# Batch 3's keys loaded behind group 1's last first-layer word, and seven more unread products in the opening of an attention and Fourier-mixing kernel

## The chip, the cores and the metric

The kernel runs on one core of one Trainium2 chip. The metric is the device time of one execution in microseconds; a kernel's time is the median of its runs. TensorE is written PE, VectorE DVE, ScalarE ACT, GpSimd POOL, and SyncE, which issues the DMA transfers, SP. PEld is PE's weight load and SPq is SP's queue.

## The reference, cut to what matters

Everything is in float32. Eight batches have 576 rows of 512 columns (eight heads of 64).

```python
q_s = softmax(q, over the 64 columns of a head)
k_s = softmax(k, over the 576 rows)
kv = einsum('bhsd,bhse->bhde', k_s, v)          # 64 x 64 per head
x = einsum('bhsd,bhde->bhse', q_s, kv)          # laid out as (8, 576, 512)
u = x + real(fft(fft(x, axis=1), axis=2))
un = (u - mean(u)) / sqrt(var(u) + 1e-6)        # over the 512 columns
out = u + relu(un @ w_ch1) @ w_ch2              # 512 -> 2048 -> 512
```

## The kernel before

**Order of the work.** Every step is a Python function with a time, in units close to a microsecond. All steps are sorted by time and recorded in that order, under a manual schedule, so each engine carries out its own instructions in the order of these times, and SP issues its transfers in that order too. A time in the code is a place in the order, not a moment on the chip. When a step really starts is set by semaphores: its operands, the buffer that it writes, and whatever stands ahead of it on its engine.

**Stages.** Batch 0 is worked off in an *opening* whose order is written out by hand in the string `OPENING`. Then come the two layers of group 0 as plain products (`plain`). While these run, the weights are put together for Strassen-like forms (seven products for eight) and written to DRAM as `w1s` and `w2s`. The groups 1 to 7 follow. Each has a first layer (`up`, products at line 1543) and a second (`down`; group 1's products are at line 1759, the others' at 1640 and 1670). While group g's layers run, the attention of the batch after it is worked off between their products.

**The opening, as far as it bears on the change.** SP loads the keys of batch 0 in four blocks, the rows shared by two batches, the queries of the tiles A to D (`own`), and the values in two halves. For each key block there is a maximum (DVE, line 553), an exponential (ACT, 556), a turn by four PE transposes (561), and a copy to SBUF (ACT, 564). `k0 last` (569) turns the last rows of all four blocks and `k0 fifth` (DVE, 572) copies them. The queries get a maximum (967), a subtraction (972, POOL or DVE), an exponential (ACT, 976), a turn (984) and a copy (995). The products of keys and values (585) need both halves of the values; `k0 scale` (DVE, 588) scales them, and the queries' products (839) need that. `t` stands for the shared rows. It has a sum and reciprocal (`t inverse`, DVE, 945 to 947), a scaling (956), a turn, folds on POOL (1017 to 1025) and products (839, 1060).

`WARM` lists unread products that are put into the opening: (time, number, columns). `warm` multiplies a block of ones by itself into a PSUM tile that nobody reads. The tile comes from `flat`, the pool `tr` of two buffers, which the transposes also use. In the opening `acc` gives a tile of the pool `two` of three buffers, which the other products use. A new tile in a pool waits until the last user of the buffer that it gets is done.

**Weights and keys in the groups.** The first layer of a group streams eight blocks of `w1s`, here called words 0 to 7, through four places in SBUF. When word n has been used, `used(n)` issues the load of word n + 4 (`load`, line 475). Words 6 and 7 are so issued as the second quarter of the first layer ends, and are needed at the start of its last quarter. `ahead(b)` puts the loads of batch b's keys (`keys_to`, four transfers, line 676), of the first half of its values (`values_to`, eight transfers, line 688) and of two query tiles at fixed times from the start of the group that runs before. Batch 3's are so loaded during group 1 and batch 4's during group 2. All are issued by SP, in one order:

```python
steps = at(20 if b == 2 else 27 if b < 5 else 24, self.keys_to(b))
steps += at(35 if b > 2 else 22.5, self.values_to(b, 0))
```

Word 6 is recorded at 27.5 of the group and word 7 at 32.5. SP waits in order: a transfer that is not yet allowed to start keeps those behind it back.

Of the kernel before, what the change touches and what calls it, by code (L numbers as in the profile page):

```python
# [46 lines left out]
P = 128  # L47
B, H, S, DH = 8, 8, 576, 64
D = H * DH
# [35 lines left out]
PAIRS = [(j + NP // 2, j) for j in range(NP // 2)]  # L85

DOWN = [(i, f) for n in range(4) for i in (2, 3, 0) for f in range(4 * n, 4 * n + 4)] + [(1, f) for f in range(NF)]
WARM = (2, 4, 256), (7.26, 1, 64), (8.52, 1, 64), (18.63, 2, 256), (22.111, 10, 256)
OPENING = """
4.30 k00 max, 5.10 k00 exp, 5.50 k01 max, 6.05 k00 turn, 6.30 k01 exp, 6.65 k02 max, 7.06 k00 four,  # L90
7.25 k01 turn, 7.56 k02 exp, 7.75 k03 max, 8.32 k01 four, 8.51 k02 turn, 8.82 k03 exp, 8.90 A max, 9.50 B max,
# [28 lines left out]
def at(t, script):  # L120
    return [(t + dt, step) for dt, step in script]
# [17 lines left out]
class _Block:  # L139
# [124 lines left out]

    def warm(self, n, cols):

        t, some = self.flat(), self.pairs[1][:].rearrange("p r n -> p (r n)")
        for _ in range(n):
            self.nc.tensor.matmul(t[:, 0:cols], lhsT=some[:, 0:P], rhs=some[:, 0:cols], start=True, stop=True)

# [258 lines left out]
    def ahead(self, b):  # L529


        steps = at(20 if b == 2 else 27 if b < 5 else 24, self.keys_to(b))
        steps += at(35 if b > 2 else 22.5, self.values_to(b, 0))
        q = [self.own_load(("q", b, 0, u)) for u in range(2)]
        if b % 2 == 0:
            q = [self.t_load(("t", b)), q[0]]
        return steps + at(46.5, q[0]) + at(50, q[1])
# [61 lines left out]
    def opening(self, fetch, converted):  # L599
# [60 lines left out]
        assert not steps, steps  # L660
        for t, *some in WARM:
            placed.append((t, lambda some=some: self.warm(*some)))
# [1330 lines left out]
```

## Time and profile before

| | us |
|---|---|
| runs | 1010.14, 1011.83, 1013.44 |
| median | 1011.83 |
| the profiled execution's own time | 1011.98 |
| its span, from first to last instruction | 1010.2 |
| PE busy in it | 995.2 (99%) |
| DVE, ACT, POOL busy | 716.1, 495.3, 443.4 |

Between the profiled execution's own time and its span lie 1.8 us, outside all instructions. In the timeline a row gives start, length, engine, line, operation, tile written and tiles read, how many records were merged, and in brackets how long the engine sat idle before it and what ended that. A float32 product shows as two records, a transpose as one. In the table by stretches each engine's busy time is given with the number of its records, and PEclk is the share of TensorE's full clock that was granted.

### The profile page before, as it was taken

What the parts mean: (1) busy time and instruction counts of PE and PEld (TensorE: products, weight loads), DVE (VectorE), ACT (ScalarE), POOL (GpSimd) and SP (SyncE); (2) the same over time, 40 slices, a digit from 0 to 9 for tenths busy, and PEclk for the clock granted to TensorE, in tenths of its full rate; (3) what the DMA queues carried; (4) which work ended last, traced back from release to release, by engine and by line L of the source; (5) the groups of instructions that cost most, each with busy time, mean ns of one, the idle gap of its engine ahead of it and who ended that gap; (6) DMA issues with size and microseconds to landing.
All of it is one profiled execution on the core that took longest, in us unless ns stands there. A gap on an engine that the chain in (4) does not pass through costs nothing.

```text
span 1010.2 us, 19785 instructions
## 1 busy us (share of the span) xinstructions
PE 995.2 (99%) x7546; PEld 855.0 (85%) x7546; DVE 716.1 (71%) x1355; ACT 495.3 (49%) x1285; POOL 443.4 (44%) x445
## 2 busy tenths in 40 slices
PE   7999999999999999999999999999999999999998
PEld 6845465888888899889988998899889998998898
DVE  6898898666665687678756887688657945685563
ACT  5685543862468128842775267725772342151210
POOL 4263420356534546664656566665646460040000
PEclk9999999999999999999999999999999999999999
DMA  8986499687999566975777577947653755674573
GB/s 299 252 292 238 170 263 314 199 240 248 326 299 241 200 245 223 244 252 208 267 215 227 208 265 248 261 168 266 226 200 147 270 200 198 224 268 180 183 251 135
DMA packets 123559, 236.37 MB, mean 234 GB/s; under 512 B 24184, under 2 KB 88440, under 8 KB 112840
## 3 DMA queue, kind: packets, MB, share of 16 engines
q1 hardware_dynamic: 123096, 234.58, 71.4%
q8 instruction: 60, 0.98, 0.4%
q10 hardware_dynamic: 288, 0.26, 0.1%
q14 instruction: 35, 0.29, 0.1%
q0 software_dynamic: 80, 0.26, 0.1%
HBM read 199.94 MB, written 39.06 MB: 237 GB/s over the span
## 4 chain that ended last, share of the span: by engine, by line
PE 84%; DVE 7%; DMA 3%; ACT 3%; issue 1%; POOL 1%; SPq 0%; DVEq 0%; POOLq 0%
PE bb L1543 15%; PE bb L1670 10%; PE ba L1543 10%; PE bc L1543 10%; PE ba L1670 7%; PE bc L1670 7%; PE bb L1640 5%; PE bc L1478 2%; PE bb L1759 2%; DMA big<-w1s 2%; ACT qT L816 2%; PE two L839 1%; PE two L1206 1%; PE two L1263 1%; PE one L754 1%; PE ba L1478 1%
## 5 line engine op out<-in xcount | busy, mean ns | idle before, releaser
L1543 PE MATMUL bb<-unT,big 128*128 128x256 f32 x768 | 184.7, 382 | 0.0
L1543 PEld LDWEIGHTS bb<-unT,big 128*128 128x128 f32 x768 | 146.0, 191 | 21.1 <-DVE u L1513 0.7
L1555 ACT ACTIVATE big<-big 128x512 f32<-128x512 f32 x96 | 59.8, 629 | 149.0 <-DVE big L1554 142.4
L1543 PE MATMUL ba<-unT,big 128*128 128x256 f32 x512 | 124.2, 383 | 2.4 <-DMA big<-w1s 2.4
L1543 PE MATMUL bc<-unT,big 128*128 128x256 f32 x512 | 121.5, 380 | 0.1
L816 ACT ACTIVATE qT<-q 32x128 f32<-32x128 f32 x384 | 117.9, 307 | 5.9 <-DVE q L806 0.8
L1543 PEld LDWEIGHTS ba<-unT,big 128*128 128x128 f32 x512 | 95.5, 190 | 16.3 <-DMA big<-w1s 2.5
L1513 DVE TENSOR_TENSOR u<-bb,s 128x512 f32<-128x512 f32 x66 | 45.2, 685 | 89.8 <-PE bb L1543 72.1
L1543 PEld LDWEIGHTS bc<-unT,big 128*128 128x128 f32 x512 | 96.9, 190 | 13.7 <-DVE big L1554 0.5
L1670 PE MATMUL bb<-big 128*128 128x128 f32 x848 | 103.9, 276 | 0.3 <-DVE u L1677 0.2
L1670 PEld LDWEIGHTS bb<-big 128*128 128x128 f32 x848 | 98.9, 192 | 1.2 <-DVE u L1677 1.2
L1389 POOL COPY unT<-unT 32x256 f32<-32x256 f32 x98 | 42.5, 434 | 90.2 <-DVE unT L1381 85.9
L1620 POOL TENSOR_TENSOR x<-x,big 128x512 f32<-128x512 f32 x45 | 61.0, 1370 | 45.9 <-DVE big L1677 19.7
L1616 DVE TENSOR_TENSOR big<-big 128x512 f32<-128x512 f32 x98 | 79.9, 843 | 0.0
L1670 PE MATMUL ba<-big 128*128 128x128 f32 x640 | 79.0, 276 | 0.0
L1670 PEld LDWEIGHTS ba<-big 128*128 128x128 f32 x640 | 75.0, 192 | 0.8
L1389 ACT COPY unT<-unT 32x256 f32<-32x256 f32 x126 | 50.7, 402 | 31.3 <-DVE unT L1381 29.5
L803 POOL TENSOR_TENSOR q<-q,qm 128x512 f32<-128x512 f32 x24 | 25.8, 1074 | 89.2 <-DVE qm L798 53.9
L404 POOL TENSOR_TENSOR big<-big 128x512 f32<-128x512 f32 x24 | 30.5, 1270 | 71.7 <-ACT big L1555 71.7
L1640 PE MATMUL bb<-big 128*128 128x256 f32 x256 | 58.3, 379 | 0.0
L1554 DVE TENSOR_TENSOR big<-bc,u 128x512 f32<-128x512 f32 x64 | 44.1, 688 | 17.0 <-PE bc L1543 16.1
L1640 PEld LDWEIGHTS bb<-big 128*128 128x128 f32 x256 | 48.0, 190 | 6.1
(335 smaller groups left out, 1912.4 us busy)
## 6 DMA issues: line engine op xcount, KB each, us to landing
big<-w2d SPq DMA_DIRECT2D x67, 1024.0 KB, 4.6
big<-w1s SPq DMA_DIRECT2D x64, 896.0 KB, 5.3
big<-w2s SPq DMA_DIRECT2D x16, 1024.0 KB, 4.8
big<-in_w_dram SPq DMA_DIRECT2D x21, 512.0 KB, 5.9
w2d<-big SPq DMA_DIRECT2D x42, 256.0 KB, 6.7
kb<-in_kT_dram SPq DMA_DIRECT2D x28, 320.0 KB, 8.3
q<-in_q_dram SPq DMA_DIRECT2D x28, 256.0 KB, 6.5
vt<-in_v_dram SPq DMA_DIRECT2D x84, 80.0 KB, 3.0
```

What stands on the lines that cost most here:

```text
L404: e1.tensor_tensor(out=to(4), in0=at(2), in1=at(3), op=ALU.add)
L816: nc.scalar.activation(to[t, i * Q:i * Q + Q], one, ACT.Exp)
L1389: copy(to, of)
L1478: nc.tensor.matmul(po[:], lhsT=h[:, f, i * P:(i + 1) * P], rhs=self.w2sb[:, f, :], start=(f == 0), stop=(f == NF - 1))
L1513: plus = lambda t: V.tensor_tensor(out=temp(t), in0=box["bb"][:], in1=box["s1"][:], op=ALU.add)
L1543: nc.tensor.matmul(bank()[:, i, :], lhsT=w[:, WA_AT[m], k * P:(k + 1) * P], rhs=self.unT[g][:, B_AT[m], k, :], start=first and i == 0 and ...
L1554: steps = [(0, lambda: V.tensor_tensor(out=hp(i), in0=bank()[:], in1=u()[:], op=ALU.add)), (0.8, lambda: nc.scalar.activation(hp(i), hp(i) ...
L1555: (0.8, lambda: nc.scalar.activation(hp(i), hp(i), ACT.Relu))]
L1616: e.tensor_tensor(out=to(o), in0=to(x), in1=to(y), op=op)
L1620: E.tensor_tensor(out=x, in0=x, in1=tile(m), op=ALU.add)
L1640: nc.tensor.matmul(box[name][:, i, :], lhsT=h[p][:, A_AT[m], i * P:(i + 1) * P], rhs=self.stream[n][:, p, :], start=p == 0 and (m != 1 or ...
L1670: nc.tensor.matmul(box[place[n]][:, i, :], lhsT=own(m)(A_AT[n])[:, f, :], rhs=w[:, r // 2, r % 2 * P:r % 2 * P + P], start=first and f == ...
```

## The change

The opening gets seven more unread products: one of 256 columns more at the start, one of 256 columns between the turns of the first two key blocks, and five of 256 columns between the turn of the last key block and that of the first query tile. All unread products of the opening write a tile of `two` in place of `tr`. The loads of batch 3's keys move from 27 to 33 in group 1. In SP's order one of the four transfers stood ahead of word 6 and the other three between words 6 and 7; now all four stand behind word 7 and ahead of the values. On ACT, DVE and POOL no instruction changes its place.

```diff
-WARM = (2, 4, 256), (7.26, 1, 64), (8.52, 1, 64), (18.63, 2, 256), (22.111, 10, 256)
+WARM = (2, 5, 256), (6.5, 1, 256), (7.26, 1, 64), (8.52, 1, 64), (10.5, 5, 256), (18.63, 2, 256), (22.111, 10, 256)
@@ def warm(self, n, cols):
-        t, some = self.flat(), self.pairs[1][:].rearrange("p r n -> p (r n)")
+        t = self.flat() if self.phase else self.acc((P, D))
+        some = self.pairs[1][:].rearrange("p r n -> p (r n)")
         for _ in range(n):
             self.nc.tensor.matmul(t[:, 0:cols], lhsT=some[:, 0:P], rhs=some[:, 0:cols], start=True, stop=True)
@@ def ahead(self, b):
-        steps = at(20 if b == 2 else 27 if b < 5 else 24, self.keys_to(b))
+        steps = at({2: 20, 3: 33, 4: 27}.get(b, 24), self.keys_to(b))
```

## The prediction

> **What bounds the kernel now.** I read the page first, then PE's waits, then the table by stretches for the clock, then the chain of waits and the timelines of the two places that the change touches.
>
> ```profile
> span 1010.2 us, 19785 instructions
> PE 995.2 (99%) x7546; PEld 855.0 (85%) x7546; DVE 716.1 (71%) x1355; ACT 495.3 (49%) x1285; POOL 443.4 (44%) x445
> ...
> PE tr L984 <- DVE q L956: 0.5, 1, 0.5
> ...
> core 0: us, PE busy (x) PEld busy (x) DVE busy (x) ACT busy (x) POOL busy (x), PEclk, DMA share, GB/s
> ...
> 5.40:10.50 5.10, 4.39 (x24) 3.27 (x24) 2.12 (x4) 3.80 (x9) 0.00 (x0) 1.00 0.83 273
> ...
> 13.40:16.80 3.40, 3.38 (x45) 2.94 (x45) 2.37 (x4) 2.74 (x5) 1.71 (x5) 0.50 0.93 316
> ...
> 42.60:174.30 131.70, 130.79 (x637) 70.00 (x638) 118.63 (x231) 71.11 (x153) 45.81 (x35) 1.00 0.80 255
> 174.30:230.00 55.70, 55.56 (x485) 47.50 (x484) 37.14 (x74) 40.42 (x117) 26.64 (x25) 1.00 0.70 207
> ...
> 327.70:330.10 2.40, 0.08 (x8) 0.00 (x0) 1.74 (x5) 0.04 (x1) 2.21 (x2) 1.00 0.56 84
> 330.10:334.30 4.20, 4.16 (x11) 3.37 (x12) 0.00 (x0) 0.59 (x1) 4.04 (x5) 0.59 0.70 221
> ```
>
> PE is busy for 99% of the span, and after 42.6 us it hardly stops. So a change pays only if PE has less to run, runs faster, or reaches 42.6 sooner. PE idles for more than 2 us in two places, and each time a stretch at a lowered clock follows: after 2.27 us that end at 12.76 (timeline below) the clock is 0.50 for 3.4 us, and after 327.7 to 330.1 it is 0.59 on average over 4.2 us. A gap therefore costs its own length and about 3.4 x 0.5 = 1.7 us of PE's work behind it. The first gap is where five of the new products go. The second is group 2's, whose keys (batch 4's) do not move. Group 1's first layer, 174.3 to 230, where the keys do move, has PE busy for 55.56 of 55.70 us.
>
> **The five products in the gap.** The opening on PE:
>
> ```profile
> 1.20 3.78 PE L269 MATMUL tr<-pairs 128*128 128x256 f32 x8 [1.20 <-DVE pairs L159]
> 5.42 1.61 PE L561 MATMUL tr<-ident,big 128*128 128x128 f32 x8 [0.44 <-POOL big L317]
> ...
> 9.84 0.66 PE L561 MATMUL tr<-ident,big 128*128 128x128 f32 x4
> 12.76 1.77 PE L984 MATMUL tr<-ident,big 128*128 128x128 f32 x8 [2.27 <-ACT big L976]
> ...
> 13.42 1.11 PE tr L984 x4
> ...
> 14.46 1.12 PE L585 MATMUL two<-big,kb 128*64 128x64 f32 x16
> ...
> 16.80 0.66 PE L984 MATMUL tr<-ident,big 128*128 128x128 f32 x4
> 17.38 0.69 PE L585 MATMUL two<-big,kb 128*64 128x64 f32 x16
> ...
> 18.70 0.66 PE L984 MATMUL tr<-ident,big 128*128 128x128 f32 x4
> ...
> 36.18 4.48 PE L269 MATMUL tr<-pairs 128*128 128x256 f32 x20
> ```
>
> Ten such products take 4.48 us at 36.18, so 0.45 each at the full clock. Four take 3.78 at the start, 0.95 each: the first ones run at half rate, though PEclk shows 1.00 there, since no change had been recorded yet. Five at full clock take 2.25 us, from 10.50 to 12.75, and the first query turn starts at 12.76. They fit the gap from 10.50 (9.84 + 0.66), and PE then never idles there. The stretch at 0.50 from 13.40 to 16.80 should go.
>
> What it is worth is read from what waits on PE there.
>
> ```profile
> 14.62 0.59 ACT L995 COPY big<-tr 128x512 f32<-128x512 f32 x1 [0.56 <-PE tr L984]
> 15.11 1.67 ACT L976 ACTIVATE big<-big 128x512 f32<-128x512 f32 x3
> ...
> 14.48 1.28 DVE L972 TENSOR_TENSOR big<-big,qm 128x512 f32<-128x512 f32 x2
> 16.81 0.69 DVE L945 TENSOR_REDUCE qrec<-big 128x8 f32<-128x512 f32 x1 [1.04 <-ACT big L976]
> ...
> 17.73 0.20 DVE L947 RECIPROCAL qrec<-qrec 128x8 f32<-128x8 f32 x1
> 18.82 0.42 DVE L588 TENSOR_TENSOR pairs<-two,kinv 128x256 f32<-128x256 f32 x1 [0.88 <-PE two L585]
> ```
>
> The turn of B starts at 13.42 either way, since ACT has its exponential ready only then, and takes 0.66 as at 16.80, not 1.11 (its piece in the chain of waits): it ends at 14.08. The first half of the key and value products takes 1.32 (17.38 to 18.70), not 2.34 (14.46 to 16.80): it ends at about 15.3. The turn of C needs its exponential. ACT copies B at 14.1 instead of 14.62, so its three exponentials start at 14.6; the last needs DVE's subtraction, done at 15.76, and ends at 16.33 instead of 16.78. That suits the turn of C at 15.3 and the second half after it, which would end at 15.3 + 0.58 + 1.32 = 17.2 if its values have landed. The trace gives no landing of them alone. By the shapes some 3.7 MB stand in SP's order up to them (keys 1.2, queries and shared rows 1.3, values 1.2), which at the 273 to 316 GB/s of the table takes 12 to 13.5 us from the start of the loads; I allow until 16, and that gives 17.3.
>
> Late next is DVE's `t inverse`: from 16.81 to 17.93 before, it follows t's exponential, so from 16.36 to 17.48. `k0 scale` stands behind it on DVE and starts at about 17.5, not 18.82. The gain on the path is 18.82 - 17.52 = 1.3 us, not the 1.7 of the clock, because the wait turns from PE to DVE. From there on the chain of waits runs through the query products, POOL's folds, DVE and PE to 42.6, all started by this; nothing in it is tied to an earlier transfer that I can see. So PE's dense part begins 1.3 us sooner, and I carry that to the end.
>
> **The two products ahead of it.** The fifth at the start costs at most 0.95, so the first key turn goes from 5.42 to 5.9 at worst. The one between the turns costs 0.45 to 0.95 more for the second.
>
> ```profile
> 7.80 0.58 ACT L564 COPY kb<-tr 128x512 f32<-128x512 f32 x1
> ...
> 11.97 0.69 DVE L572 COPY big<-tr 64x512 f32<-64x512 f32 x1
> ```
>
> The second turn ended at 7.03 (5.42 + 1.61) and its copy starts only at 7.80, when ACT is done with the third block's exponential. That 0.77 covers most. Uncovered, the last key turn goes from 9.84 to 10.5 and the five products end at 13.4: 0.7 lost. Nearest are the rows with slack, so I take 0.0 to 0.2. The query turn has a bound besides PE: the buffer that `k0 fifth` frees at 12.66.
>
> **The other pool.** Two old products now write a buffer of `two` that tile B's output (DVE) must first have read.
>
> ```profile
> 22.68 1.13 PE L269 MATMUL tr<-pairs 128*128 128x256 f32 x4
> 22.76 0.69 DVE L875 TENSOR_TENSOR x<-two,qrec 128x512 f32<-128x512 f32 x1
> ...
> 23.79 0.68 POOL L1025 TENSOR_TENSOR F<-T 128x272 f32<-128x272 f32 x1
> 24.53 0.69 PE L839 MATMUL two<-pairs,F 64*64 64x64 f32 x32 [0.72 <-DVE x L875]
> ```
>
> They ran at 22.68. Now they wait until 23.45 and run 0.9 us to about 24.4. Behind them on PE are the products at 24.53, which need POOL's fold, done at 24.47. So it is free by 0.1 us; without that cover it costs at most 0.4. I take 0.
>
> **The keys.** On SP and PE in group 1, and the one slow word of group 2:
>
> ```profile
> 201.32 0.33 SPq L475 DMA_DIRECT2D big<-w1s  x1
> 201.70 1.70 SPq L676 DMA_DIRECT2D kb<-in_kT_dram  x3
> 203.50 0.44 SPq L475 DMA_DIRECT2D big<-w1s  x1
> 203.99 12.19 SPq L688 DMA_DIRECT2D vt<-in_v_dram  x8
> 216.28 0.85 SPq L475 DMA_DIRECT2D big<-w2s  x2
> ...
> 218.43 1.13 PE L1543 MATMUL ba<-unT,big 128*128 128x256 f32 x4
> ...
> 313.99 16.11 DMA big<-w1s
> ...
> 330.14 1.44 PE L1543 MATMUL ba<-unT,big 128*128 128x256 f32 x4 [2.36 <-DMA big<-w1s]
> ```
>
> Word 7 goes from 203.50 to about 202, when the products that free its place end, and it no longer shares the DMA with three key transfers issued just ahead. PE first needs it at 218.43, where no wait stands, so there is nothing to save here. The four transfers now pass both words; behind them on SP are eight value transfers, the first second-layer loads (216.28, needed when the second layer starts at 230, the end of that stretch in the table) and two query tiles. The bytes are the same, so the end of the stretch stays near 216; batch 3's keys are not read before group 2. Cost 0; bounds: a gain of 4.1 (below) and a loss if second-layer words came 9 us later.
>
> **The sum**, against the profiled execution: 1011.98 - 1.3 = 1010.7 us. That execution lies 0.15 above the median of the runs, 1011.83, so it holds for that too (-0.1%).
>
> **The rivals.**
>
> *No gain.* Either the cold stretch was not in most runs of before, or the 1.3 us is lost between 42.6 and 174.3, where DVE is busy for 118.63 of 131.70 us and PE once waits 0.5 us for it. Against it: that wait stands at the end of a DVE chain which starts from PE's own turns. Time 1011.9. [...]
>
> *Much faster.* In other runs word 7 is late in group 1 as it was in group 2, where it took 16.11 us; 203.50 + 16.11 is 1.2 us past 218.43. Then the reordering takes away up to what group 2 pays, 2.4 + 1.7 = 4.1 us, beside the 1.3: 1006.6. Against it: the profiled run has no such wait.
>
> *Slower, the five run cold.* The place is 10.50. If the clock has already dropped before it, five products take 4.7 us and the query turn starts at 15.2 instead of 12.76; the point from which this decides is any start later than 10.5 or any rate below 0.45. What follows is then at full clock, which gives back part: at worst +2.0, 1014.0. Against it: 5.40 to 10.50, nearly all transposes, shows 1.00. [...]
>
> *Slower, a new stall.* The second-layer words of group 1, behind the keys and values, come past 230. Price as in group 2: 4.1, 1014.8 after the gain, 1016.1 without it. It needs 9 us of delay, which nothing shows.
>
> **How the numbers follow.** Forecast 0.46, no gain 0.19, much faster 0.18, cold products 0.09, new stall 0.08. A measurement of this kernel can tell about 0.3% (3 us) from no change. Faster by more than that, under 1008.8, is the third case and a seventh of the first two for scatter, since three runs of before lie 3.3 us apart: 0.26. Slower, over 1014.9, is the new stall and some scatter of the cold case: 0.12. The same: 0.62. The range runs from 1006.8, just above the middle of the much faster case, to 1013.8, which leaves out the stall.
>
> **What would show it.** In the profile after: PE busy without a gap from 9.8 to 19, the five products in 2.2 to 2.4 us, granted clock 1.00 from 13.4 to 16.8, `k0 scale` near 17.5 and waiting no longer for PE, first-layer products of group 0 at about 41.3 instead of 42.63, and group 1's last-quarter products still without a wait. It is wrong if the five take over 4 us, if the scaling stays at 18.8, if the lead is gone by 174, or if group 1 shows a wait for w1s or w2s.

## The result and the profile after

| | kernel before | kernel after |
|---|---|---|
| median of 13 runs each | 1009.63 us | 1007.09 us |
| lowest to highest | 1007.66 to 1015.26 | 1006.09 to 1008.77 |
| ratio, 95% interval | | 0.9976 [0.9966, 0.9986] |
| profiled execution, its span | 1011.98, 1010.2 | 1008.46, 1006.7 |

The change saves 0.24% of the time [0.14%, 0.34%], 2.4 us. The forecast was a saving of 1.3 us, 0.13%, just under this interval. The saving is below the 0.3% that the prediction took for the least to be told from no change, and 1007.09 lies in its range, near the lower end; but the forecast time itself, 1010.7, stood on the first three runs of before, which lay high: the ten further ones have a median of 1009.3. The range held the result by its width. The profiled executions differ by more than the medians, and mostly not by what the change does, as follows.

The page of after:

```profile
span 1006.7 us, 19811 instructions
PE 995.8 (99%) x7560; PEld 856.1 (85%) x7560; DVE 717.8 (71%) x1355; ACT 494.9 (49%) x1285; POOL 443.2 (44%) x445
```

PE is busy for 995.8 us where it was for 995.2, with 14 records more: the gain is idle time and clock, not work. The table by stretches of after (PEclk is the third column from the right):

```profile
13.40:16.80 3.40, 3.37 (x74) 2.82 (x74) 2.70 (x6) 3.18 (x7) 1.70 (x5) 1.00 0.93 314
...
20.04:23.45 3.41, 1.31 (x72) 1.08 (x64) 1.59 (x7) 1.85 (x9) 3.05 (x7) 1.00 1.09 381
23.45:26.86 3.41, 3.33 (x52) 2.52 (x52) 3.09 (x9) 0.00 (x0) 0.00 (x0) 0.50 1.09 380
...
203.00:226.00 23.00, 22.96 (x268) 19.59 (x267) 13.64 (x27) 16.38 (x46) 12.47 (x10) 1.00 1.01 276
```

The stretch from 13.40 to 16.80 runs at 1.00 with 74 records, where before had 0.50 and 45. But in this execution a stretch of the same length at 0.50 lies ten microseconds later, behind one in which PE was busy for only 1.31 of 3.41 us. The timelines of PE and DVE in after say why:

```profile
9.87 0.66 PE L562 MATMUL tr<-ident,big 128*128 128x128 f32 x4
10.36 2.32 PE L270 MATMUL two<-pairs 128*128 128x256 f32 x10
12.91 1.31 PE L985 MATMUL tr<-ident,big 128*128 128x128 f32 x8 [0.22 <-issue]
...
19.45 0.85 PE L840 MATMUL two<-pairs,big 64*64 64x65 f32 x41
21.62 1.04 PE L840 MATMUL two<-pairs,big 64*64 64x65 f32 x55 [1.32 <-issue]
23.54 2.04 PE L270 MATMUL two<-pairs 128*128 128x256 f32 x4 [0.87 <-DVE qrec L862]
...
43.71 1.97 PE L1467 MATMUL ba<-unT,big 128*128 128x256 f32 x8 [0.88 <-ACT eo L1326]
```
```profile
17.53 0.20 DVE L948 RECIPROCAL qrec<-qrec 128x8 f32<-128x8 f32 x1
17.76 0.42 DVE L589 TENSOR_TENSOR pairs<-two,kinv 128x256 f32<-128x256 f32 x1
```

The five products fit their gap: 2.32 us from 10.36, and A's turn follows at 12.91, after 0.22 us of idle time. The scaling of k0 starts at 17.76, 1.06 sooner, right behind the reciprocal of t and without a wait for PE. Then two idle pieces appear. PE stops 1.32 us between the 41st and the 55 other records of the query products, for nothing that the profile shows, and 0.87 us ahead of the two products that now use the pool `two`, until DVE has read tile B's output (that ends at 23.39; the row names the short instruction right behind it). With the slower clock behind them the lead is gone: group 0's first layer starts at 43.71, after 42.63 in before.

The same stop was in before, shorter:

```profile
20.51 1.04 PE L839 MATMUL two<-pairs,big 64*64 64x65 f32 x55
21.90 0.85 PE L839 MATMUL two<-pairs,big 64*64 64x65 f32 x41 [0.35 <-issue]
```

In group 1 the keys moved as the change says, on SP, and PE waits for nothing:

```profile
202.03 1.19 SPq L476 DMA_DIRECT2D big<-w1s  x2
203.27 3.13 SPq L677 DMA_DIRECT2D kb<-in_kT_dram  x4
206.44 10.72 SPq L689 DMA_DIRECT2D vt<-in_v_dram  x8
217.37 0.82 SPq L476 DMA_DIRECT2D big<-w2s  x2
```
```profile
219.13 1.13 PE L1544 MATMUL ba<-unT,big 128*128 128x256 f32 x4
```

From group 1's first product to its second layer PE takes 55.84 us in both kernels. So where do the 3.5 us between the two spans come from? Group 2's first layer took 58.9 us in the profile of before and 54.7 in that of after. That is the wait of 2.36 us for a word and the slow clock behind it, which the prediction showed and which the change does not touch. In this pair of traces the opening lost 1.1 us, group 0 gave back 0.4 (131.3 us instead of 131.7 from its first layer to group 1), and the wait that happened not to occur gave 4.2.

### The profile page after: what moved, and what is told of

Same layout as the page of the kernel before. It is cut to its first block, busy times and chain, and to the rows that moved or that the text cites. A ratio compares the mean times of both kernels' runs of the same rounds, so it can differ in the third digit from the quotient of the medians.

```text
span 1006.7 us, 19811 instructions
## 1 busy us (share of the span) xinstructions
PE 995.8 (99%) x7560; PEld 856.1 (85%) x7560; DVE 717.8 (71%) x1355; ACT 494.9 (49%) x1285; POOL 443.2 (44%) x445
## 4 chain that ended last, share of the span: by engine, by line
PE 88%; DVE 7%; ACT 3%; DMA 1%; issue 1%; SPq 0%; POOL 0%; DVEq 0%; POOLq 0%; ACTq 0%
PE bb L1544 16%; PE ba L1544 11%; PE bc L1544 11%; PE bb L1671 10%; PE ba L1671 7%; PE bc L1671 7%; PE bb L1641 5%; PE bc L1479 2%; PE bb L1760 2%; PE two L840 2%; PE one L755 2%; PE two L1207 1%; PE two L1264 1%; PE ba L1479 1%; PE bc L1760 1%; PE ba L1760 1%
## 5 line engine op out<-in xcount | busy, mean ns | idle before, releaser
L1390 ACT COPY unT<-unT 32x256 f32<-32x256 f32 x126 | 50.7, 402 | 31.3 <-DVE unT L1382 29.5
```

Of the source, the lines that this page charges most:

```text
L1390: copy(to, of)
```

## The experiments

Two theories stand against each other. By the first, the opening carries the gain: the five products keep the clock at 1.00, and the lead is partly taken back by the stop in the query products. By the second, it is the keys, or the words of group 2. The table holds the profiled execution of each kernel: start of A's turn, of the scaling of k0 and of group 0's first layer (line 1466 in before), the time from the first of these to the last, the length of group 2's first layer, and the span, all in us; then the ratio to before over all runs.

| kernel | A's turn | k0 scale | first layer | turn to layer | group 2 | span | ratio [95%] |
|---|---|---|---|---|---|---|---|
| before | 12.76 | 18.82 | 42.63 | 29.87 | 58.9 | 1010.2 | 1 |
| e1 keys only | 13.34 | 20.32 | 44.06 | 30.72 | 55.0 | 1007.1 | 1.0000 [0.9988, 1.0012] |
| e9 batch 4's keys only | 13.44 | 20.29 | 44.44 | 31.00 | 54.9 | 1008.7 | 0.9988 [0.9975, 1.0000] |
| after | 12.91 | 17.76 | 43.71 | 30.80 | 54.7 | 1006.7 | 0.9976 [0.9966, 0.9986] |
| e11 after again | 12.18 | 17.04 | 41.43 | 29.25 | 54.7 | 1004.5 | 0.9979 [0.9968, 0.9989] |
| e2 opening only | 12.88 | 17.75 | 42.06 | 29.18 | 54.8 | 1004.9 | 0.9984 [0.9975, 0.9993] |
| e3 two in tr | 13.39 | 18.25 | 42.64 | 29.25 | 54.8 | 1005.8 | 0.9981 [0.9972, 0.9990] |
| e4 both batches' keys | 13.40 | 18.26 | 42.64 | 29.24 | 54.7 | 1006.4 | 0.9978 [0.9968, 0.9989] |
| e10 e3 and e4 | 12.53 | 17.39 | 42.03 | 29.50 | 54.7 | 1005.6 | 0.9978 [0.9968, 0.9989] |
| e7 five only | 12.68 | 17.54 | 41.70 | 29.02 | 55.8 | 1006.2 | 0.9991 [0.9979, 1.0003] |
| e12 two products | 12.88 | 17.74 | 41.82 | 28.94 | 54.7 | 1005.1 | 0.9981 [0.9971, 0.9991] |
| e5 words held | 13.24 | 18.10 | 41.86 | 28.62 | 55.3 | 1006.1 | 0.9989 [0.9976, 1.0002] |
| e6 twenty small | 14.28 | 18.80 | 43.07 | 28.79 | 54.9 | 1006.5 | 0.9992 [0.9983, 1.0002] |
| e8 ten products | 14.95 | 19.47 | 43.33 | 28.38 | 56.7 | 1008.9 | 0.9990 [0.9981, 0.9998] |

The start of A's turn scatters by 1.2 us between executions of the same opening (12.18 to 13.40), so the differences are read from it on. Each ratio is to runs of before on the same chip: e1 to e4 ran on one, e5 to e8 on a second, e9 to e12 on a third. After stands beside them on the third alone (e11); e5 to e8 all lie at 0.9989 to 0.9992, and a difference of 0.001 between them and after may be the chip's.

**e1, the keys alone.** The kernel before with one line changed.

```diff
-        steps = at(20 if b == 2 else 27 if b < 5 else 24, self.keys_to(b))
+        steps = at({2: 20, 3: 33, 4: 27}.get(b, 24), self.keys_to(b))
```

> Only batch 3's keys move (33 for 27); the opening is that of before. Theory 'opening' (the prediction's): no difference from before, ratio 0.999 to 1.001, since the profiled run of before shows no wait for a word in group 1. Theory 'keys': group 1's word 7 does come late in other runs of before, so this alone gives most of the change's 2.5 us: ratio 0.997 to 0.9985, and the slowest runs of before (1012 and more) are missing here. In both, the opening shows the cold stretch and the first-layer products of group 0 start near 42.6.

1009.37 us beside 1009.87 of before. The keys' move alone brings nothing: 0 within 1.2 us either way. Its opening has two stretches at 0.50 one behind the other:

```profile
9.03:12.45 3.42, 1.31 (x8) 0.84 (x8) 1.95 (x4) 0.84 (x4) 1.21 (x2) 1.00 0.87 303
12.45:15.86 3.41, 2.52 (x20) 2.22 (x22) 3.35 (x7) 2.57 (x6) 2.52 (x6) 0.50 0.99 314
```

**e2, the opening alone.** The change without that line.

> Only the opening changes (seven more products, all in the other pool); batch 3's keys stay at 27. Theory 'opening': 1.0 to 2.5 us faster than before, ratio 0.9975 to 0.999. Theory 'keys': no difference, ratio 0.9995 to 1.001, because PE's lead of 1.06 us at the scaling is taken back by PE's own instruction fetch near 20 to 22 us: PE stops in the middle of the query products (after 41 records of 96, where it was 55 before) until about 21.6, whatever its lead; the lead behind it is 0.3 us at most.

1007.71 us on the same chip, 0.16% less than before. By the medians the opening carries two thirds of the 0.24%; its interval allows 0.07% to 0.25%, so the whole gain too. No stretch at 0.50, and 29.18 us from the turn to the layer.

**e3, the moved products back in `tr`.** Only the two at 18.63 change their pool.

```diff
-        t = self.flat() if self.phase else self.acc((P, D))
+        t = self.flat() if self.phase or n == 2 else self.acc((P, D))
```

> The changed kernel, but the two unread products at 18.63 write a tile of the pool tr again, so that they don't wait for tile B's output. If that wait costs time, PE's idle time before them (0.87 us at 23.54 in the changed kernel's profile) goes, the shared rows' products start near 24.3 instead of 25.5, and the median is 0.3 to 1.0 us under the changed kernel's 1007.1. If it is covered as the prediction had it, the median is the changed kernel's within 0.3 us and only the place of the idle time differs.

1007.53 us. The wait of 0.87 for DVE goes, a stop of 0.6 us comes elsewhere, and the layer starts 29.25 us behind the turn as in e2 and e4, which have the wait. So the wait for the pool by itself costs nothing here.

**e4, batch 4's keys behind word 7 of group 2 too.**

```diff
-        steps = at({2: 20, 3: 33, 4: 27}.get(b, 24), self.keys_to(b))
+        steps = at({2: 20, 3: 33, 4: 33}.get(b, 24), self.keys_to(b))
```

> The changed kernel with batch 4's keys moved as well (33 for 27), behind group 2's words. If the wait for a word in group 2 (2.4 us in the profiled run of before, none in that of the changed kernel) is an event that comes in some runs, it comes in none here: median 0 to 1 us under the changed kernel's 1007.1, no run above 1008.5 but for the opening. If it was a rarity: no difference. Slower by up to 1 us would mean that batch 4's keys or values come too late.

1007.44 us: not to be told from after.

**e5, the words held back.** The opening's eleven loads of weight words, and batch 1's keys and values, are issued only behind a store of tile A's x.

```diff
+        hold = self.dram.tile([P, D], F32, tag="hold", name="hold", bufs=1)
+        words = [lambda: load(hold[:], self.xpart(0, 0, 0)), *(lambda i=i: fetch(i) for i in range(11))]
...
+        return ([(i / 100, step) for i, step in enumerate(order)] + [(18.501 + i / 1000, step) for i, step in enumerate(words)]
```

> The changed kernel, with the loads of the eleven opening weight words, and batch 1's keys and values after them, issued only once tile A's x has been stored to a scratch tile in DRAM: few transfers move while PE's instructions of the query products are fetched. Theory 1 (PE stops near the 450th record since a 16 KB packet of its instructions is fetched late, and the word loads slow that fetch): the stop, 1.32 us with the change and 0.35 before, shrinks to 0.3 or less, the first-layer products of group 0 come 28.6 us or less behind the start of A's turn instead of 29.2, and the time is about 0.5 us under the changed kernel's, 1006.6 where that has 1007.1. Theory 2 (PE stops for something else, a semaphore or a limit of its own): the stop stays at 0.9 to 1.4 us and the time does not fall. In both, the words come about 6 us later; if group 0's first layer then waits for them, its start moves to over 30 us behind A's turn and the kernel is 1 us or more slower.

The stop has nearly gone: on PE the 96 records run in one piece. The transfers by queue from 18.1 to 19.3 us (packets, MB, share of 16 engines) are a packet of instructions and little else:

```profile
19.80 1.88 PE L843 MATMUL two<-pairs,big 64*64 64x65 f32 x96
```
```profile
q8 instruction: 1, 0.02, 5.2%
q1 hardware_dynamic: 9, 0.01, 1.5%
```

The layer came 28.62 us behind the turn, as the first theory expected. But the time is 1008.36. In the profiles group 0 took 131.9 us where e11 took 131.1, and group 2's first layer 55.3 where it took 54.7; that the late words did this is likely, but no run separates it. What is shown is that the stop ends 1.3 to 1.4 us behind the end of the packet: it comes at 19.60 us in before and at 19.39 in after, takes 0.9 us in both, and the stop ends at 21.90 and 21.62 (e6, below, is the third case). That the loads slow the fetch is not shown: the packet takes 1.0 us here, no less than in after with all loads running. It comes at 18.20 here, but in e11, with all loads too, the stop ended at 20.48, which puts its packet at about 18.2 (an estimate, 1.4 and 0.9 us before that). Against e11, A's turn came 1.06 us later here and the packet, by this estimate, at the same time, which by itself makes the stop shorter.

**e6, twenty products of 64 columns for the five.**

```diff
-WARM = ..., (10.5, 5, 256), ...
+WARM = ..., (10.5, 20, 64), ...
```

> The changed kernel with twenty products of 64 columns in place of the five of 256 columns between the last key turn and A's turn: the same columns, 30 more PE instructions with a weight load and two records each for every product. Theory 1 (the stop lies at a fixed number of PE instructions): PE stops after about as many records as before, near 450, and so 30 to 60 records earlier in the work, among or ahead of the first query products, and goes on when the fetch is done. Theory 2 (the stop belongs to a certain product of the work): it stays behind the 41st record of the query products. The time: the twenty take 2.4 to 3 us, so that A's turn comes up to 0.7 us later; 1007 to 1008.5.

1008.86 us; the twenty took 4.4 us, not 2.4 to 3: 0.22 each, where one of 256 columns takes 0.45. There is no stop at the query products. It comes later on PE, at the products of t, and the transfers by queue from 23.6 to 24.6 us show the packet ahead of it:

```profile
25.02 0.29 PE L1061 MATMUL two<-pairs,F 64*64 64x64 f32 x6
25.98 0.44 PE L1061 MATMUL two<-pairs,F 64*64 64x64 f32 x10 [0.68 <-issue]
```
```profile
q8 instruction: 1, 0.02, 5.5%
```

So the stop does not belong to a product of the work. What it belongs to is seen by counting PE's records from the start to the stop in the table by stretches (first and second count: products and weight loads). In order: before, after, e7 and e6.

```profile
0.00:21.80 21.80, 16.92 (x219) 13.12 (x219) 12.50 (x25) 12.44 (x25) 8.91 (x27) 0.92 0.86 285
```
```profile
0.00:21.00 21.00, 17.91 (x219) 14.34 (x220) 12.52 (x25) 12.70 (x26) 9.15 (x28) 1.00 0.85 283
```
```profile
0.00:20.50 20.50, 17.78 (x219) 14.41 (x220) 12.54 (x25) 12.39 (x25) 8.87 (x27) 1.00 0.89 296
```
```profile
0.00:25.60 25.60, 21.71 (x346) 18.29 (x346) 16.21 (x35) 13.94 (x32) 11.47 (x32) 1.00 0.93 312
```

It comes behind the 219th record of a product wherever it comes at the query products, and in e6 behind the 346th: 127 records of products and as many of weight loads later, 254 together. The page of before has 60 packets on the queue of instructions over the whole run (below; those of after and e9 to e12 have 60 too), 0.98 MB or 16 KB each. It has 7546 records of products on PE and as many of weight loads, 15092 together, or 252 to a packet. So the packets are probably PE's, and PE stops where it has used up one of them and the next has not come. That is an estimate from these counts; the trace does not name the engine that a packet is for. PE idled there for 1.32 us in after, 0.35 in before and 0.68 in e6.

```profile
q8 instruction: 60, 0.98, 0.4%
```

**e7, the five products alone**, without the fifth at the start, the one at 6.5 and the keys' move.

```diff
-WARM = (2, 5, 256), (6.5, 1, 256), (7.26, 1, 64), ...
+WARM = (2, 4, 256), (7.26, 1, 64), ...
```

> The kernel before with the five products ahead of A's turn and the pool of the unread products changed, but without the fifth product at the start, without the one at 6.5 and with batch 3's keys where they were. Theory 1 (the five keep the clock and carry the whole gain): ratio to before 0.998 to 0.9985, as the whole opening alone had 0.9984, A's turn to the scaling of k0 in about 4.85 us. Theory 2 (the two products ahead are needed for the clock to stay through 6.5 to 13): a stretch at clock 0.50 remains in the opening of most runs, the mean granted clock of a run stays near 0.997, and the ratio is 0.999 to 1.000.

Between the two: 1008.13 us, with 3 of 12 runs at a mean clock of 0.998 or less. (Of the 67 runs of the kernels that have all seven products, 3 are so low.) From the turn to the layer the profile has 29.02; a wait of 1.0 us for a word in group 2 lengthens its span. Two products less ahead put the stop four records later, behind 45 instead of 41, which is what a count of instructions asks for, as each product has two records. So it is in e12, with three products less (47), and in before, with seven less (55):

```profile
19.23 0.92 PE L840 MATMUL two<-pairs,big 64*64 64x65 f32 x45
20.78 1.03 PE L840 MATMUL two<-pairs,big 64*64 64x65 f32 x51 [0.63 <-issue]
```

Whether the two products ahead bring anything stays open; they cost nothing that shows.

**e8, ten products in place of five.**

```diff
-WARM = ..., (10.5, 5, 256), ...
+WARM = ..., (10.5, 10, 256), ...
```

> The changed kernel with ten products instead of five ahead of A's turn: 2.25 us more work, in a gap that the five fill. A's turn comes about 2.2 us later. Theory 1 (what the lead is worth is capped by the stop near the 450th record, which ends only when the instructions are there, about 21.6): of the 2.2 us the stop gives back up to 1.3, so the time is 0.9 to 1.6 us above the changed kernel's. Theory 2 (nothing gives way): 2.2 us above it, as slow as the kernel before or slower.

1008.18 us, a ratio 0.0014 above that of after, or 1.4 us, as the first theory has it, though on another chip. The profile agrees: the layer starts at 43.33, where it lies between 41.43 and 42.64 with five products and no cold stretch. A's turn comes 2.0 us later than in after, and 28.38 us on to the layer are the shortest of all: PE has reached its 219th record at 21.7 us, when the stop of after had ended (21.62), and does not stop there. What the stop took in the others is given back.

**e9, batch 4's keys alone in the kernel before.**

```diff
-        steps = at(20 if b == 2 else 27 if b < 5 else 24, self.keys_to(b))
+        steps = at({2: 20, 3: 27, 4: 33}.get(b, 24), self.keys_to(b))
```

> The kernel before with one line changed: the loads of batch 4's keys at 33 of group 2 instead of 27, so that all four stand behind word 7. The opening and batch 3's keys are as before. Theory 1 (group 2's wait for a first-layer word, 2.36 us with a stretch at clock 0.50 behind it in the profile of before, comes in many runs of before): word 7 is issued 2 us earlier, the wait goes in all runs, the median falls by 1 us or more (ratio 0.998 to 0.999) and the highest runs come down. Theory 2 (that wait is an accident of few runs): the ratio is 0.9995 to 1.0005. In both, group 2 takes 54.8 us from its start to its second layer in the profile.

Inconclusive: the interval holds both expectations. The medians are 1009.5 and 1009.3; the highest run is 1010.5, that of before 1014.6. The wait for a word in group 2 stood in 3 of 14 profiles (2.36 in before, 1.0 in e7, 1.9 in e8), never where batch 4's keys had moved (e4, e9, e10). Three profiles are too few to tell that from chance, and e9 has a wait of 0.7 us for a word in group 4.

**e10, e3 and e4 together.**

> The changed kernel with both side effects taken out: the two unread products between the query products stay in the pool tr, and batch 4's keys are loaded at 33 as well. Theory 1 (the pool's wait and group 2's wait cost the changed kernel something in the median): ratio to before 0.996 to 0.997, 0.5 to 1 us under the changed kernel on the same chip. Theory 2 (neither wait decides its median): within 0.4 us of it. In the profile no stretch at clock 0.50 in the opening, 29.2 us from A's turn to the first-layer products of group 0, 54.8 us for group 2's first layer.

1007.29 us: neither wait decides the median, the second theory. It is no better than after.

**e11, after once more.**

> The changed kernel once more, unchanged, so that it stands on the same chip beside the others. Every theory: ratio to before 0.997 to 0.9985. If its profile has a wait for B's output at the moved products of 0.9 us and the stop of the query products together, theory 1 (these two make the clock's window idle) expects the stretch at clock 0.50 behind 23 us again; theory 2 (that stretch was an accident of where the window fell) expects clock 1.00 throughout.

1006.92 us, 0.9979: the result stands. Its profile has both idle pieces, 0.91 and 0.86 us, and yet 1.00 throughout. They fell on two sides of the clock's grid of 3.41 us (windows counted from the moment at which the trace first shows the full clock; that is 6.55 us in before and 6.38 in after, and their stretches at 0.50 begin two and five windows on, at 13.38 and 23.45):

```profile
18.12:21.53 3.41, 2.50 (x108) 2.09 (x100) 1.79 (x7) 2.13 (x9) 1.89 (x6) 1.00 1.09 378
21.53:24.95 3.42, 2.56 (x57) 2.14 (x58) 3.29 (x8) 0.73 (x3) 1.15 (x2) 1.00 1.09 385
```

In after they fell into one window, 20.04 to 23.45, with 1.31 us of work in it. Falling into one window is not enough, though. In e4 the two pieces, 0.89 and 0.87 us, lie in one window too, and the clock holds, here and in the window behind it:

```profile
20.10:23.51 3.41, 1.75 (x96) 1.52 (x93) 2.02 (x7) 2.30 (x9) 2.64 (x7) 1.00 1.09 381
23.51:26.92 3.41, 3.31 (x63) 2.90 (x64) 3.27 (x10) 1.26 (x4) 0.40 (x1) 1.00 1.09 376
```

So the second theory, with a condition: the stretch came where both pieces fell into one window and the stop was at its longest, 1.32 us. The place of the window differs between the two executions of this kernel: one begins at 20.04 in after, others at 18.12 and 21.53 in e11. By the mean clock (0.998), 2 of the 13 runs of after had such a stretch, the profiled one among them, and none of the 12 of e11.

**e12, two products in place of five.**

```diff
-WARM = ..., (10.5, 5, 256), ...
+WARM = ..., (10.5, 2, 256), ...
```

> The changed kernel with two products instead of five ahead of A's turn: 0.9 us of work in a gap of 2.3 us, so PE idles 1.4 us there. Theory 1 (what counts is that the window is busy enough, and 1.4 us of 3.4 idle is still enough): clock 1.00 from 13 to 17, A's turn to the scaling of k0 in 4.85 us, and the time of the changed kernel within 0.5 us. Theory 2 (the gap must be filled): in some runs a stretch at clock 0.50, mean clock of a run near 0.998, and the time half way to before, ratio 0.9985 to 0.9995.

1006.92 us, the first theory by the median: PE idles 1.28 us and the clock stays at 1.00, as it does by the mean clock (0.999 or more) in 9 of 11 runs. The other two, with 0.998, are the slowest, 1008.77 and 1009.04, and are what the second theory expected of some runs. The window around the gap in the table by stretches, and A's turn on PE:

```profile
10.03:13.45 3.42, 2.09 (x12) 1.49 (x12) 3.32 (x7) 1.60 (x3) 2.04 (x2) 1.00 0.86 233
```
```profile
12.88 0.63 PE L985 MATMUL tr<-ident,big 128*128 128x128 f32 x4 [1.28 <-ACT big L977]
```

Beside it the same window of before:

```profile
9.97:13.38 3.41, 1.14 (x8) 0.70 (x8) 3.31 (x7) 1.63 (x3) 2.04 (x2) 1.00 0.79 244
13.38:16.79 3.41, 3.38 (x45) 2.93 (x44) 2.38 (x4) 2.74 (x5) 1.71 (x5) 0.50 0.93 314
```

## Why the prediction was right or wrong

- **The clock and the five products: right.** 2.32 us in the gap, 1.00 from 13.40 to 16.80. PE was idle for 0.22 us at 12.91 and 0.21 at 18.24, where no gap was forecast. None of the ten profiles with five or more products there, nor that of e12 with two, has a stretch at 0.50 between 10 and 20 us; the three with the old opening all have one. The rival of five cold products fell: e8 ran ten in 4.48 us.
- **The scaling of k0: right.** From A's turn it came at 4.85 us instead of 6.06, 1.21 sooner where 1.3 was taken, and the reciprocal of t is what it follows, as was said.
- **The carrying of the lead to 42.6: wrong, and it is the step that failed.** "Nothing in it is tied to an earlier transfer that I can see" overlooked the stop at PE's 219th record, by the counts above a fetch of its own instructions, though its sign, 0.35 us of "issue" at 21.90, stood in the trace of before. Without cold stretches the layer comes 29.2 to 29.5 us behind the turn, 0.4 to 0.7 sooner than in before and not 1.3. In after the cold stretch at 23.45 took even that: group 1 begins at 174.99 after 174.28 in before, so that the lead is gone by 174, which the prediction named as a sign of being wrong. What took the lead is seen from the scaling of k0 to the layer. That time is 23.5 us plus the length of the stop, within 0.05, in nine profiles: before (stop 0.35, time 23.81), e12 (0.62, 24.08), e7 (0.63, 24.16), e9 (0.70, 24.15), e2 (0.81, 24.31), e3 and e4 (0.89, 24.39 and 24.38), e11 (0.91, 24.39) and e10 (1.16, 24.64). Whether the pool's wait is there or not makes no difference. Where the stop is short or missing, 23.7 to 23.9 remain (e1, e5, e8); e6, whose stop comes later, has 24.27, and after, with its cold stretch, 25.95. So the work that came 1.2 us sooner met a stop longer by 0.5 to 0.8.
- **What made up for it: a term set too low.** The prediction gave the old opening one cold stretch. The profiles of e1 and e9 have two, 6.82 us, and 30.72 and 31.00 from turn to layer. Over the three profiles of the old opening that is 30.5 on average, over e2, e3, e4, e10 and e11 29.3: 1.2 us, or 1.0 if after's 30.80 is taken in. The 1.3 of the sum was nearly right as an average by luck, for a reason that the sum didn't hold.
- **The pool: priced at zero, found at 0.87 us idle.** It costs nothing by itself (e3, e10), but it is 0.8 of the 2.1 us of idle time in the window ahead of the stretch at 0.50 in after's profile. Its bound of 0.4 left that out.
- **The keys: right.** Zero in group 1, and in e1 zero within 1.2 us. The rival "much faster" had the mechanism, late words, in the wrong group.
- **No gain: wrong.** Some runs of before seem to have no cold stretch, as 26 of 99 had a mean clock of 0.999 or more, but most seem to have one. The gain is there. The rival's other half, a loss between 42.6 and 174.3, did not come: that stretch took 131.7 us in before and 131.1 to 131.5 in the six profiles with the whole new opening.

**What stays open.** The medians of after and e11 lie 2.5 and 2.4 us under those of before; the opening up to group 0 explains 1.0 to 1.2. The mean clock points to more: 0.9977 over the 99 runs of before beside e1 to e12, 0.9999 over those of e11. One stretch is 3.41 x 0.5 = 1.7 us, or 0.0017, so 1.3 stretches a run went, 2.2 us of PE's work. But among the 99, the 26 with hardly any cold stretch have a median of 1009.38 and the 42 at 0.997 or less one of 1009.94; the clock alone does not order them. One reason may be that the mean counts the start at full clock (PEclk 1.00 from 0 to 5.5 us), where the first five products took 4.63 us in after and 4.33 in e2, which have the same opening, and ten took 4.48 later. No run separates that. Rare stalls are not the whole rest: between all 112 runs of before and the 67 of the kernels with the whole new opening, 2.3 us apart at the median, the upper ends of the lowest tenths still lie 1.7 us apart (the lower ends of the highest tenths 3.0).

## What to carry to other kernels

Unread products need not fill a gap: here two, with PE busy for 2.09 of the 3.42 us of the window around it, gave the median that five gave (1006.92 us), with a mean clock of 0.998 left in 2 of 11 runs. Before carrying a lead through a dense stretch, look in it for "issue" idle of PE with a packet of instructions just ahead; here the work that came 1.2 us sooner waited there 0.5 to 0.8 longer. And compare stage by stage from a common start: two profiled executions differed here by 3.5 us, and a stall that the change does not touch made 4.2 by itself.

## What the runs showed of the hardware

- **Clock.** In before, e1, e9 and after PEclk fell to 0.50 for a window of 3.41 us, or for two on end (e1, e9: 6.82). In the window ahead PE was busy for 1.14 and 1.06 us (before, the opening and group 2), 1.31 (e1), 1.06 (e9) and 1.31 (after). Windows in which it was busy for 1.75 (e4), 2.09 (e12) and 2.50 us (e11) had 1.00 behind them. Of the windows at 0.50, those with 2.52 (e1) and 2.23 us (e9) had a second one behind them, and those with 3.33 (after) and 3.38 (before) had 1.00. In before the two stretches begin at 13.38 and 330.82 us, 317.44 apart, which is 93 times 3.413: the windows of this execution lie on one grid. It lies differently in others: windows begin at 9.97 in before, at 9.03 in e1 and at 8.84 in e9, which have the same opening.

```profile
8.84:12.26 3.42, 1.06 (x7) 0.56 (x5) 1.70 (x3) 0.49 (x2) 0.92 (x1) 1.00 0.92 310
12.26:15.67 3.41, 2.23 (x14) 1.93 (x16) 3.31 (x7) 2.42 (x5) 2.59 (x7) 0.50 0.95 303
15.67:19.08 3.41, 3.41 (x52) 2.96 (x50) 1.83 (x5) 2.19 (x5) 0.22 (x1) 0.50 1.05 379
```

  These are the three windows of e9: the first with 1.06 us of work, the second at half clock with 2.23, the third at half clock too.
- **Instructions.** PE stopped behind its 219th record of a product in ten of the fourteen profiles for 0.35 to 1.32 us, and in e6 and e8 behind the 345th or 346th for 0.68 and 0.76. In before, after and e6 the stop ended 1.3 to 1.4 us behind the end of a packet of 16 KB on the queue of instructions, which took 0.9 us there, with the DMA full, and 1.0 in e5, where it was not.
